# A fused attention and gated-MLP kernel: q projections begun ten units earlier, and longer DMA times in its schedule

## The chip, the cores and the metric

The kernel runs on one core of a Trainium2 chip. The metric is the device time of one execution in microseconds (us). The core's engines have queues of their own, each worked off in order: TensorE (PE; its weight loads are shown apart as PEld), VectorE (DVE), ScalarE (ACT), GpSimd (POOL), and SyncE (SP), which here only issues DMAs. They meet at semaphores.

## What is computed

For a sequence of 2048 rows of width 512, a layer norm, and then the sum of the input, an attention block of 32 heads of width 16, and an MLP gated by a ReLU, with F = 1792:

```python
qkv = x @ wqkv                       # 32 heads, 16 wide
scores = jnp.einsum("bhqd,bhkd->bhqk", q, k) * (Dh ** -0.5)
p = _softmax(scores, axis=-1)
o = jnp.einsum("bhqk,bhkd->bhqd", p, v)
...
h = (gate * (gate > 0)) * up
...
return x + _A_ref(xn, A_wqkv, A_wo) + _B_ref(xn, B_W_gate, B_W_up, B_W_down)
```

The softmax is over all 2048 keys of each of 32 heads, so there are 32 x 2048 x 2048 exponentials. They are what most of the kernel's time is arranged around.

## The kernel before

**Blocks and units.** The queries are cut into 4 pieces of 512 (`c4`), the heads into 4 groups of 8 (`gg`), and each group into two halves (`ee`) of four heads. A block is one (c4, gg, ee), and there are 32; two blocks with the same c4 and gg share one q projection and are called a pair here, numbered 0 to 15. For each block and each of the 16 key tiles of 128 there are four score tiles (one per head, 128 keys by 512 queries). Most of these tiles are gathered into units of three and two in turn: TensorE writes a unit's scores into one of two PSUM buffers (`ps_sc`, L1193), ScalarE takes the exponential of the whole unit in one instruction (L1260, into `ring`). There are 647 units. They are the clock of the schedule: dates in it are unit numbers.

**The share of VectorE.** 108 of the groups of four score tiles do not go to ScalarE. TensorE writes their scores to a PSUM bank of `ps_b`, and VectorE computes their exponentials in several instructions (L1209 from PSUM, then L1220, L1222, L1224, L1225 in SBUF, into `dring`). Which places of a block these groups take is listed in `D_POS`; how many units ahead of its place such a group is begun is `D_LEAD`.

**PV.** `pv_group` (L1149) multiplies the exponentials with v (L1169) into bank 0 of `ps_b`. Its rank in the schedule is its unit plus `PV_LAG`. The row of sums comes out of the same product, from a column of ones.

**q.** `proj_q` (L749) multiplies normalised rows with a slice of Wq into bank 1 of `ps_b`. VectorE copies the result to `qT` (L778, one buffer). Then three DMAs bring it into the layout of the scores: a write to `q_scr` in HBM (L782) and two reads into `qm` (L785, three buffers), one for each half. Pair 0 takes another way, without DMAs. A job per pair is wanted 36 units ahead of the pair's start (L1002).

**o.** `normalise` (L1089) works when a block's PV is done: VectorE copies the sums and products to `o_sb`, which lies in the storage of Wv (the profile calls it Wv, L1103); a DMA fetches the row sums into `rsum` (L1120); POOL inverts them (L1121); two DMAs bring the inverses to HBM and, repeated over partitions, back into `rb` (L1123, L1126); POOL multiplies in four parts (L1131); a DMA writes the result to `o_scr` (L1139); and after the second half of a pair one more DMA reads it back in the layout of the output product (L1145, into `oT` or into slots of `x_sb`). `out_rows` (L948) uses it, with the MLP's last product (both L726).

**MLP.** `glu` (L920) loads slices of the up and gate weights (L927, L928), multiplies (L726) and lets VectorE form h (L933, L937). The MLP, the projections and the output rows are jobs spread over the units by `spread` (L1003), whose pace is scaled by `TIGHT`. Most of these products share bank 1 of `ps_b`.

**What sets the order.** Nothing is reordered on the chip. `Graph.run` (L164) makes, when the kernel is built, one list per engine from assumed durations (`dur`), times until a result can be used (`lat`) and priorities. An operation with a date is not put ahead of that unit. For a DMA, `dur` is SP's issue and `lat` the time from there until a reader can use the data. A reader is placed where the list expects its data to be there. `SLIP` and `HOLD` are tolerances, in ns, for POOL's multiplications beside VectorE's work and for VectorE's score tiles. Where TensorE would stand idle too much, `blanks` (L257) puts in fillers: matmuls with zeros (L1310). `Graph.emit` (L349) then writes the lists out with semaphore waits. A real DMA that takes longer than its `lat` does not change the order; the engine that reads it stops there, with everything behind it.

Of the kernel before, what the change touches and what calls it, by code (L numbers as in the profile page):

```python
# [17 lines left out]
DH = 16  # L18
# [9 lines left out]

SIZES = (3, 2)
NRING = 6  # L30
PV_LAG = 2.0
PV_MIN = 0
NWS = 3
NQ = 3
NDR = 9
KD = (1, 5, 9, 13)
D_LEAD = 9.0
D_POS = (
    (), (2, 3, 8, 12), (2, 8, 11, 15), (4, 8, 11),
    (2, 6, 12), (1, 5, 9, 15), (5, 10, 14), (2, 5, 10, 11),  # L40
    (2, 3, 15), (1, 3, 4, 10), (5, 9, 15), (2, 3, 7, 12),
    (4, 6, 11), (2, 5, 9, 11), (2, 7, 12), (4, 9, 10, 13),
    (5, 10, 11), (1, 8, 9, 10), (6, 7, 10, 11), (3, 6, 13),
    (1, 8, 11, 14), (4, 8, 14), (8, 12, 15), (2, 7, 14, 15),
    (1, 8, 14), (3, 4, 11), (1, 6, 10, 13), (1, 7, 13),
    (1, 8, 10), (2, 10, 11), (1, 2, 7, 14), (1, 2, 5, 9),
)
D_BANKS = (2, 1)
D_SEQ = 0
D_AHEAD = 5  # L50
D_WAIT = 1.0
# [12 lines left out]
F_PRE = (1, 1, 1)  # L64
F_BEG = 20
F_END = 18
TIGHT = 1.0
EV = -16.0

LOG2E = 1.4426950408889634  # L70
# [31 lines left out]
class Graph:  # L102
# [2 lines left out]

    ENGS = ("PE", "ACT", "DVE", "POOL", "SP")
    SWITCH = 100.0
    SLIP = 100.0
    KEEP = 4.0
    RIDE = 100.0  # L110
    HOLD = 500.0
    WINDOW = 3400.0
    FILL = 0.72
    BLANK = 216.0
# [336 lines left out]
def bass_parallel_sum__mha_block__glu_gated_reglu__prompt_kernel(  # L451
# [16 lines left out]
    with ExitStack() as es:  # L468
        def sb(name, shape, dt):
# [35 lines left out]
        rsum = sb("rsum", [128, 2, 16], FP32)  # L505
# [32 lines left out]
             reads=[t_pid], writes=[t_pid], prio=-890)  # L538
        G.op("DVE", 100, lambda e: e.tensor_scalar(hmask[:, 1:2], pid[:, 0:1], 1.0 / 16.0, None, op0=ALU.mult),
             reads=[t_pid], writes=[t_mask], prio=-889)  # L540
        G.op("DVE", 100, lambda e: e.tensor_scalar(hmask[:, 0:1], pid[:, 0:1], -1.0 / 16.0, 1.0, op0=ALU.mult, op1=ALU.add),
             reads=[t_pid], writes=[t_mask0], prio=-888)
# [4 lines left out]
             reads=[t_id], writes=[t_id], prio=-898)  # L547
        t_vones, t_woz, t_minus = Tile(), Tile(), Tile()
        G.op("POOL", 200, lambda e: e.memset(minus[:], -1.0), writes=[t_minus], prio=10)
        t_qz = [Tile(), Tile()]  # L550
# [6 lines left out]
             reads=[t_id32], writes=[t_id32], prio=60)  # L557
# [6 lines left out]
        def dma(fn, kb, writes=(), reads=(), prio=0.0, stream=None, order=(), name="dma", after=None, dur=370.0, lat=None):  # L564
            o = G.op("SP", dur, fn, reads=reads, writes=writes, prio=prio, stream=stream or ("o", len(G.ops)),
                        lat=2000 if lat is None else lat, order=order, name=name, after=after)
            o.kb = kb if lat is None else 0.0
            return o

        x_src = x2.rearrange("(m p) d -> p m d", p=128)  # L570
        for i in range(2):
            dma(lambda e, i=i: e.dma_start(q_scr[i, :, DH:2 * DH, :], qT[:, 0, :]), 128,
                reads=[t_qt0], writes=[t_qz[i]], prio=-600)
# [35 lines left out]
        for j in range(4):  # L609
            for ee in range(2):  # L610
                dma(lambda e, j=j, ee=ee: e.dma_start(Wo_p[32 * j:32 * j + DH, ee, :], wo_src[NGG - 1, j, ee, :, :]), 16,
                    reads=[t_woz], writes=[Tile()], prio=40)
# [136 lines left out]
        def proj_q(c4, gg, prio=0.0, tile=None, sub=0, eng="DVE", slots=None):  # L749
            t = tile or Tile("pq", P_b, [1])  # L750
            prio = slots[-1] if slots else prio
            if (c4, gg) == (0, 0):
                for c0 in range(0, 384, 128):
                    first_chain(t, sub, Wq, t_wq[0], prio, c0, c0 + 128)
                first_chain(t_pro[1], 0, Wq, t_wq[0], prio, 384, 512)
            else:
                mm_chain(t, [((lambda dt=dt: Wq[:, dt, 128 * gg:128 * gg + 128]), (lambda dt=dt: xnT[:, dt, 512 * c4:512 * c4 + 512]))
                             for dt in range(DT)], [t_wq[gg], t_xnT[c4]], prio, sub=sub, slots=slots)
            tq = t_q[(c4, gg)] = Tile("q", P_q)
            if eng == "ACT":  # L760
                for tt, sb, c0, c1, up in ((t, sub, 0, 384, 0.0), (t_pro[1], 0, 384, 512, -20.0)):
                    n = (c1 - c0) // 128
                    G.op("ACT" if n == 3 else "DVE", 190 + 105 * n if n == 3 else 230, (lambda e, tt=tt, sb=sb, c0=c0, c1=c1: e.activation(
                        qm[:, tq.slot, 0, c0:c1], bank_of(tt, sb)[:, c0:c1], ACTF.Copy, scale=hmask[:, 0:1])) if n == 3 else (lambda e, tt=tt, sb=sb, c0=c0, c1=c1: e.tensor_scalar(
                        qm[:, tq.slot, 0, c0:c1], bank_of(tt, sb)[:, c0:c1], hmask[:, 0:1], None, op0=ALU.mult)),
                        reads=[tt, t_mask0], writes=[tq] if n == 3 else [t_q4], prio=prio + up)
                    o = G.ops[-1]
                    if n == 1:
                        tq.w.append(o)
                        t_after.append(o)  # L770
                    o = G.op("DVE", 100 + 130 * n, lambda e, tt=tt, sb=sb, c0=c0, c1=c1: e.tensor_scalar(
                        qm[:, tq.slot, 1, c0:c1], bank_of(tt, sb)[:, c0:c1], hmask[:, 1:2], None, op0=ALU.mult),
                        reads=[tt, t_mask], writes=[t_q1], prio=prio + 1.5)
                    o.deps[tq.w[-1]] = True
                    tq.r.append(o)
            else:
                tr = Tile("qr", P_qr)
                G.op("DVE", 610, lambda e: e.tensor_copy(qT[:, tr.slot, :], bank_of(t, sub)), reads=[t], writes=[tr], prio=prio)  # L778
                par = (4 * c4 + gg) % 2
                tqs = Tile("qs")  # L780
                tqs.r.extend(q_last[par])
                dma(lambda e: e.dma_start(q_scr[par, :, 0:DH, :], qT[:, tr.slot, :]), 128,  # L782
                    reads=[tr] + t_qz, writes=[tqs], prio=prio - 60, stream=("qw", par), dur=500, lat=2400)
                for ee in range(2):
                    dma(lambda e, ee=ee: e.dma_start(qm[:, tq.slot, ee, :], q_pick(par, ee)), 128,  # L785
                        reads=[tqs], writes=[tq] if ee == 0 else [], prio=prio - 60 + 0.1 * ee, stream=("qr%d" % ee, par), dur=500, lat=2700)
                o = G.ops[-1]
                o.order.add(tq.w[0])
                tq.w.append(o)
                q_last[par] = G.ops[-2:]  # L790
# [73 lines left out]
        def upos(c4, gg=0, ee=0, kt=0):  # L864
            x = (c4 * NGG + gg) * 2 + ee + kt / NT
            i = min(int(x), len(blocks) - 1)
            return int(starts[i] + (starts[i + 1] - starts[i]) * (x - i))
# [27 lines left out]
        o_sb = Wv[:, :, :].rearrange("p a b -> p (a b)").bitcast(FP32).rearrange("p (s q) -> p s q", s=2)  # L895
# [97 lines left out]
        def job(want, n, fn, lead=10, pace=1.0):  # L993
            jobs.append((want, n, fn, lead, pace))
# [4 lines left out]
        for c4 in range(NB):  # L999
            for gg in range(NGG):  # L1000
                if (c4, gg) != (0, 0):
                    job(upos(c4, gg) - 36, 2, lambda s, c4=c4, gg=gg: proj_q(c4, gg, slots=s))  # L1002
        def spread(a, z, items, extra):  # L1003
            pace = (z - a) / (sum(n for n, _, _, _ in items) + extra)
            pos, step = a, (z - a) / sum(n for n, _, _, _ in items)
# [22 lines left out]
        for want, n, fn, lead, pace in jobs:  # L1028
            s = []
# [10 lines left out]
        t_os, o_last = {}, [[], []]  # L1040
# [48 lines left out]
        def normalise(c4, gg, ee):  # L1089
            g = 2 * gg + ee  # L1090
            n = c4 * 8 + g
            tp = pv_tile[(c4, gg, ee)]
            to = Tile("o", P_o)
            if n == 4 * 8 - 1:
                for h in range(2):
                    o = G.op("DVE", 350, lambda e, h=h: e.tensor_copy(o_sb[:, to.slot, 256 * h:256 * h + 256], ps_b[:, 0, 256 * h:256 * h + 256]),
                             reads=[tp], writes=[to] if h == 0 else [], prio=-950, name="oev%d" % n)
# [6 lines left out]
            pr = upos(c4, gg, ee, NT) + 1  # L1104
            if (c4, gg, ee) == (NB - 1, NGG - 1, 0):
                tn, ts, tr = Tile("oT", P_oT), Tile("ls", P_b, [1]), Tile("lr", P_b, [1])
                spread_sums(lambda a, b: o_sb[:, to.slot, a:b], 0, 4, 0, lambda a, b: ps_b[:, 1, a:b], lambda p, c: ps_b[p:p + 32, 1, c:c + 128], to, ts, tr, pr + 80)
                G.op("DVE", 610, lambda e: e.tensor_tensor(oT_of(tn), ps_b[:, 1, :], o_sb[:, to.slot, :], ALU.mult),
                     reads=[tr, to], writes=[tn], prio=pr - 900)
# [6 lines left out]
            par = n % 2  # L1116
            if n >= 2:
                ts.r.extend(last_rec[n - 2][0].r)
                trr.r.extend(last_rec[n - 2][1].r)
            dma(lambda e: e.dma_start(rsum[:, par, :], o_sb[DH:128:32, to.slot, :]), 8, reads=[to], writes=[ts], prio=pr - 50, stream=("n1", n % 4), dur=600, lat=2600)  # L1120
            G.op("POOL", 3000, lambda e: e.tensor_tensor(rrec[:, par, :], rsum[:, par, :], minus[:, 0:1].to_broadcast([128, 16]), ALU.pow),  # L1121
                 reads=[ts, t_minus], writes=[trr], prio=pr - 50)
            dma(lambda e: e.dma_start(rec_scr[n].rearrange("j (i q) -> (j i) q", q=16), rrec[:, par, :]), 8,  # L1123
                reads=[trr], writes=[tsc], prio=pr - 50, stream=("n2", n % 4), dur=340, lat=1600)
            last_rec[n] = (ts, trr)
            dma(lambda e: e.dma_start(rb[:, trb.slot, :], rec_scr[n].unsqueeze(1).to_broadcast([4, 32, 512])), 256,  # L1126
                reads=[tsc], writes=[trb], prio=pr - 50, stream=("n3", n % 4), dur=580, lat=5300)
            tn = Tile("oT", P_oT)
            for k in range(N_MUL):
                w = 512 // N_MUL  # L1130
# [6 lines left out]
            tos = t_os[(c4, gg, ee)] = Tile("os")  # L1137
            tos.r.extend(o_last[par])
            dma(lambda e: e.dma_start(o_scr[par, :, ee, :, :], oT_of(tn)), 128,  # L1139
                reads=[tn], writes=[tos], prio=pr - 50, stream=("ow%d" % ee, par), dur=500, lat=2400)  # L1140
            if ee:
                tw = t_oT[(c4, gg)] = Tile("oT", P_oT)
                t = o_scr[par, :, :, :, :]
                src = bass.AP(tensor=t.tensor, offset=t.offset, ap=[(32 * 512, 8), (512, DH), (1, 512)])
                dma(lambda e: e.dma_start(oT_of(tw), src), 128,  # L1145
                    reads=[t_os[(c4, gg, 0)], tos], writes=[tw], prio=pr - 50, stream=("or", par), dur=500, lat=2600)
                o_last[par] = [G.ops[-1]]

        def pv_group(key, kt, u):  # L1149
# [206 lines left out]
```

## Time and profile before

| what | value |
|---|---|
| median of 7 runs | 776.55 us (775.56 to 779.59) |
| profiled execution | 776.03 us, of which the span of the profile is 774.2 us |
| granted TensorE clock, mean | 0.999 |
| VectorE L1209, scores from PSUM | 432 instructions, 291.6 us busy |
| GpSimd (POOL) | 162.4 us busy, 21% |
| DMA | 46.83 MB in 95757 packets, mean 60 GB/s |

The profile shows one execution. Times within it are counted in us from the start of its span. In a row of costliest groups, the figures behind the bar are the time the group was busy, the mean of one in ns, and, behind the second bar, how long the engine stood idle just before these instructions, with what ended most of that idle time. The chain of waits follows the work that ended last, back from the end: each line is a start, a length, and what it was, either an instruction or a DMA under way. A line that begins with DMA runs from its issue to the moment where its reader could go on. In the windows view a line gives a stretch, its length, the engine's busy time with the count of instructions, the TensorE clock, the share of the DMA engines and the GB/s.

### The profile page before, as it was taken

The numbers are of one execution on the slowest core, as the hardware profiler recorded it, in microseconds if no ns is written. First come the engines' busy times: TensorE is split into PE (matmuls) and PEld (weight loads), VectorE is DVE, ScalarE is ACT, GpSimd is POOL, SyncE is SP. The second block draws the span as 40 slices with busy tenths as digits, with TensorE's granted clock in tenths as the row PEclk, the third lists the DMA queues.
The fourth block names the chain that finished last, engine by engine and source line by source line (L and its number), as shares of the span: only waits on it lengthen the run. The fifth ranks groups of instructions, "written<-read, shape, count | busy, mean of one in ns | idle before, by whom it ended". The sixth has DMA issues, their size and how long they took to land.

```text
span 774.2 us, 21504 instructions
## 1 busy us (share of the span) xinstructions
PE 748.8 (97%) x9446; PEld 227.8 (29%) x9446; DVE 736.5 (95%) x1148; ACT 748.8 (97%) x662; POOL 162.4 (21%) x172
## 2 busy tenths in 40 slices
PE   8999999999999999999999999999999999999997
PEld 3322222222222322232232222222232322232333
DVE  8799999999999899999998999999999989899997
ACT  6999999999999999999999999999999999999994
POOL 3102112220212221221222021223122232121200
PEclk9999999999999999999999999999999999999999
DMA  7402121312102122232301112222230212221100
GB/s 225 134 16 60 51 62 30 78 36 64 53 28 60 48 67 57 59 82 62 84 24 56 43 49 77 57 66 67 64 81 25 63 44 66 76 69 57 36 15 29
DMA packets 95757, 46.83 MB, mean 60 GB/s; under 512 B 69936, under 2 KB 91824, under 8 KB 95664
## 3 DMA queue, kind: packets, MB, share of 16 engines
q1 hardware_dynamic: 95664, 45.46, 21.5%
q8 instruction: 74, 1.21, 0.6%
q14 instruction: 19, 0.16, 0.1%
HBM read 36.70 MB, written 8.50 MB: 58 GB/s over the span
## 4 chain that ended last, share of the span: by engine, by line
DVE 45%; PE 44%; DMA 4%; ACT 4%; issue 1%; SPq 0%; POOL 0%; DVEq 0%
DVE dring L1209 17%; PE ps_b L726 16%; PE ps_b L1169 12%; PE ps_sc L1193 12%; DVE dring L1224 7%; DVE dring L1220 4%; ACT ring L1260 4%; DVE dring L1225 4%; DVE dring L1222 4%; PE ps_b L1193 3%; DVE up_sb L933 2%; DMA qm<-q_scr 2%; DVE hT L937 2%; DVE Wv L1103 1%; DMA q_scr<-qT 1%
## 5 line engine op out<-in xcount | busy, mean ns | idle before, releaser
L1260 ACT ACTIVATE ring<-ps_sc 128x1536 bf16<-128x1536 f32 (+1 forms) x647 | 740.4, 1256 | 9.0 <-PE ps_sc L1193 4.2
L1209 DVE TENSOR_SCALAR dring<-ps_b 128x512 uint16<-128x512 f32 x432 | 291.6, 685 | 17.8 <-PE ps_b L1193 16.3
L1193 PE MATMUL ps_sc<-qm,kT 32*128 32x512 bf16 x1616 | 259.6, 384 | 2.8 <-ACT ring L1260 1.4
L1193 PE MATMUL ps_b<-qm,kT 32*128 32x512 bf16 x432 | 163.7, 384 | 6.5 <-DMA qm<-q_scr 3.1
L1169 PE MATMUL ps_b<-ring,v_aug 128*17 128x512 bf16 x1616 | 144.3, 381 | 4.4 <-DVE Wv L1103 3.4
L1121 POOL TENSOR_TENSOR rrec<-rsum,minus 128x16 f32<-128x16 f32 x30 | 96.3, 3211 | 223.9 <-DMA rsum<-Wv 223.9
L1224 DVE TENSOR_TENSOR dring<-dring 128x2048 bf16<-128x2048 bf16 x108 | 131.4, 1217 | 0.0
L1193 PEld LDWEIGHTS ps_sc<-qm,kT 32*128 32x128 bf16 x1616 | 62.0, 91 | 223.5 <-ACT ring L1260 182.1
L1131 POOL TENSOR_TENSOR x_sb<-Wv,rb 128x128 bf16<-128x128 f32 x100 | 45.9, 462 | 283.4 <-DVE dring L1220 59.7
L1169 PE MATMUL ps_b<-dring,vd 128*17 128x512 bf16 x864 | 80.6, 382 | 0.8 <-DVE dring L1224 0.2
L1169 PE MATMUL ps_b<-dring,v_aug 128*17 128x512 bf16 x864 | 78.6, 381 | 0.3
L1220 DVE TENSOR_SCALAR dring<-dring 128x2048 uint16<-128x2048 uint16 x108 | 73.9, 688 | 0.6
L1225 DVE TENSOR_SCALAR dring<-dring 128x2048 uint16<-128x2048 uint16 x108 | 73.9, 687 | 0.0
L1222 DVE TENSOR_SCALAR dring<-dring 128x2048 uint16<-128x2048 uint16 x108 | 73.8, 686 | 0.0
L726 PE MATMUL ps_b<-xnT,wus 128*32 128x512 bf16 x896 | 69.2, 384 | 1.2 <-DVE dring L1209 0.2
L726 PE MATMUL ps_b<-xnT,wgs 128*32 128x512 bf16 x896 | 68.7, 384 | 0.7 <-DVE up_sb L933 0.4
L1169 PEld LDWEIGHTS ps_b<-ring,v_aug 128*17 128x17 bf16 x1616 | 37.2, 89 | 61.0 <-issue 36.4
L1193 PEld LDWEIGHTS ps_b<-qm,kT 32*128 32x128 bf16 x432 | 38.7, 91 | 49.9 <-DVE dring L1209 27.3
L726 PE MATMUL ps_b<-Wd,hT 128*32 128x512 bf16 x672 | 48.9, 382 | 0.0
L933 DVE COPY up_sb<-ps_b 128x512 f32<-128x512 f32 x56 | 38.3, 684 | 2.2 <-PE ps_b L726 2.1
L1169 PEld LDWEIGHTS ps_b<-dring,vd 128*17 128x17 bf16 x864 | 20.5, 89 | 37.7 <-DVE dring L1225 10.9
L1169 PEld LDWEIGHTS ps_b<-dring,v_aug 128*17 128x17 bf16 x864 | 20.4, 89 | 33.1 <-issue 16.9
(109 smaller groups left out, 378.9 us busy)
## 6 DMA issues: line engine op xcount, KB each, us to landing
rb<-rec_scr SPq DMA_DIRECT2D x30, 256.0 KB
wus<-in_B_W_up_dram SPq DMA_DIRECT2D x56, 128.0 KB, 2.8
wgs<-in_B_W_gate_dram SPq DMA_DIRECT2D x56, 128.0 KB, 2.4
qm<-q_scr SPq DMA_DIRECT2D x30, 128.0 KB
o_scr<-x_sb SPq DMA_DIRECT2D x25, 128.0 KB
q_scr<-qT SPq DMA_DIRECT2D x17, 128.0 KB
xr_sb<-in_A_x_dram SPq DMA_DIRECT2D x16, 128.0 KB, 3.3
out_dram<-xn_sb SPq DMA_DIRECT2D x16, 128.0 KB, 1.7
```

Of the source, the lines that this page charges most:

```text
L726: ins = e.matmul(bank_of(tile, sub)[32 * j:32 * j + 32, :], st[:, 32 * j:32 * j + 32], mv, start=(i == 0), stop=(i == n - 1), tile_positio ...
L933: G.op("DVE", 610, lambda e: e.tensor_copy(up_sb[:, tup.slot, :], bank_of(tu)), reads=[tu], writes=[tup], prio=slots[1] + EV)
L1121: G.op("POOL", 3000, lambda e: e.tensor_tensor(rrec[:, par, :], rsum[:, par, :], minus[:, 0:1].to_broadcast([128, 16]), ALU.pow), reads=[t ...
L1131: o = G.op("POOL", 200 + 1080 // N_MUL, lambda e, a=w * k, b=w * k + w: e.tensor_tensor(oT_of(tn)[:, a:b], o_sb[:, to.slot, a:b], rb[:, tr ...
L1169: ins = e.matmul(ps_b[32 * j:32 * j + VN, 0, :], v, src[j][1](k), start=(first and k == 0), stop=(last and k == ways - 1), tile_position=( ...
L1193: return e.matmul(bank, kT[32 * j:32 * j + 32, gg, 128 * kt:128 * kt + 128], qm[32 * j:32 * j + 32, t_q[(c4, gg)].slot, ee, :], start=True ...
L1209: o = G.op("DVE", 610, lambda e, j=j, ts=ts: e.tensor_scalar(dring[:, tp.slot, 512 * j:512 * j + 512].bitcast(U16), ps_b[:, ts.slot, :], 0 ...
L1220: G.op("DVE", 600, lambda e: e.tensor_scalar(b(tm, U16), b(tp, U16), 0xFF80, None, op0=ALU.bitwise_or), reads=[tp], writes=[tm], prio=u - ...
L1222: G.op("DVE", 600, lambda e: e.tensor_scalar(b(tn, U16), b(tp, U16), 0xFF80, 1, op0=ALU.bitwise_and, op1=ALU.bitwise_or), reads=[tp], writ ...
L1224: G.op("DVE", 1140, lambda e: e.tensor_tensor(b(tm), b(tp), b(tm, I16), ALU.mult), reads=[tm, tp], writes=[tm], prio=u - 3, name="d5", loc ...
L1225: G.op("DVE", 600, lambda e: e.tensor_scalar(b(ts_, U16), b(tp, U16), float(SHIFT), None, op0=ALU.add), reads=[tp], writes=[ts_], prio=u - ...
L1260: return e.activation(ring[:, a:a + n, :], ps_sc[:, 3 * k0:3 * k0 + n, :], ACTF.Exp, scale=0.25)
```

## The change

Two named constants are new. `Q_LEAD = 46` takes the place of the number 36 in the date of the q jobs. `LATE = 900` is added to `lat` of the DMAs that TensorE's operands pass through: the write and the reads of q, the read into `rb`, and the write and the read of o. Half of it is added for the row sums and for their inverses on the way out. Other values that the lists are made from change with them: `PV_LAG`, `D_LEAD`, `TIGHT`, `SLIP`, `HOLD` and entries of `D_POS` (none of whose lists gets longer or shorter).

```diff
-PV_LAG = 2.0
+PV_LAG = 1.0
...
-D_LEAD = 9.0
+D_LEAD = 10.0
 D_POS = (
-    (), (2, 3, 8, 12), (2, 8, 11, 15), (4, 8, 11),
+    (), (2, 3, 8, 12), (2, 8, 11, 15), (4, 9, 11),
...
 D_BANKS = (2, 1)
+Q_LEAD = 46
+LATE = 900
...
-TIGHT = 1.0
+TIGHT = 0.97
...
-    SLIP = 100.0
+    SLIP = 60.0
...
-    HOLD = 500.0
+    HOLD = 400.0
...
# proj_q
                 dma(lambda e: e.dma_start(q_scr[par, :, 0:DH, :], qT[:, tr.slot, :]), 128,
-                    reads=[tr] + t_qz, writes=[tqs], prio=prio - 60, stream=("qw", par), dur=500, lat=2400)
+                    reads=[tr] + t_qz, writes=[tqs], prio=prio - 60, stream=("qw", par), dur=500, lat=2400 + LATE)
...
-  stream=("qr%d" % ee, par), dur=500, lat=2700)
+  stream=("qr%d" % ee, par), dur=500, lat=2700 + LATE)
...
# the list of jobs
-                    job(upos(c4, gg) - 36, 2, lambda s, c4=c4, gg=gg: proj_q(c4, gg, slots=s))
+                    job(upos(c4, gg) - Q_LEAD, 2, lambda s, c4=c4, gg=gg: proj_q(c4, gg, slots=s))
...
# normalise: rsum, rec_scr, rb, o_scr, oT
-  stream=("n1", n % 4), dur=600, lat=2600)
+  stream=("n1", n % 4), dur=600, lat=2600 + LATE // 2)
...
-  stream=("n2", n % 4), dur=340, lat=1600)
+  stream=("n2", n % 4), dur=340, lat=1600 + LATE // 2)
...
-  stream=("n3", n % 4), dur=580, lat=5300)
+  stream=("n3", n % 4), dur=580, lat=5300 + LATE)
...
-  stream=("ow%d" % ee, par), dur=500, lat=2400)
+  stream=("ow%d" % ee, par), dur=500, lat=2400 + LATE)
...
-  stream=("or", par), dur=500, lat=2600)
+  stream=("or", par), dur=500, lat=2600 + LATE)
```

No instruction's operands change. The orders of the engines do, and the number of filler matmuls goes from 168 to 216.

## The prediction

> **What bounds the kernel now.** I read the page's busy shares first, then the costliest groups, then ScalarE's idle time, and last the chain around each stall.
>
> ```profile
> PE 748.8 (97%) x9446; PEld 227.8 (29%) x9446; DVE 736.5 (95%) x1148; ACT 748.8 (97%) x662; POOL 162.4 (21%) x172
> L1260 ACT ACTIVATE ring<-ps_sc 128x1536 bf16<-128x1536 f32 (+1 forms) x647 | 740.4, 1256 | 9.0 <-PE ps_sc L1193 4.2
> L1193 PEld LDWEIGHTS ps_sc<-qm,kT 32*128 32x128 bf16 x1616 | 62.0, 91 | 223.5 <-ACT ring L1260 182.1
> ```
>
> Three engines are nearly full, so shares alone decide nothing. The second row is one exponential per unit: 740.4 us over 647 units is 1.144 us of ScalarE per unit. The third says that TensorE's score loads stood 182.1 us waiting for ScalarE to free a score bank: TensorE is the faster one, held to ScalarE's pace. ScalarE sets the end, and what can be gained in mid-kernel is its idle time. The windows view of ScalarE in three undisturbed stretches (length, busy):
>
> ```profile
> 75.00:420.00 345.00, 343.98 (x303) 1.00 0.21 55
> 430.00:660.00 230.00, 228.77 (x201) 1.00 0.22 57
> 715.00:755.00 40.00, 39.81 (x36) 1.00 0.09 25
> ```
>
> It idles 2.44 us in 615. The rest of its mid-kernel idle time is in four places, shown by its timeline (start, length, idle before in brackets):
>
> ```profile
> 64.86 1.02 ACT L1260 ACTIVATE ring<-ps_sc 128x1024 bf16<-128x1024 f32 x1 [0.75 <-PE ps_sc L1193]
> 66.16 1.45 ACT L1260 ACTIVATE ring<-ps_sc 128x1536 bf16<-128x1536 f32 x1 [0.28 <-PE ps_b L1193]
> ...
> 424.79 3.82 ACT L1260 ACTIVATE ring<-ps_sc 128x1536 bf16<-128x1536 f32 x3 [1.51 <-PE ps_b L1193]
> ...
> 666.33 3.46 ACT L1260 ACTIVATE ring<-ps_sc 128x1024 bf16<-128x1024 f32 x3 [0.89 <-PE ps_sc L1193]
> 670.01 2.37 ACT L1260 ACTIVATE ring<-ps_sc 128x1536 bf16<-128x1536 f32 x2 [0.22 <-PE ps_sc L1193]
> ...
> 706.72 1.03 ACT L1260 ACTIVATE ring<-ps_sc 128x1024 bf16<-128x1024 f32 x1 [0.80 <-PE ps_sc L1193]
> 708.24 2.37 ACT L1260 ACTIVATE ring<-ps_sc 128x1536 bf16<-128x1536 f32 x2 [0.49 <-PE ps_sc L1193]
> ```
>
> 0.75+0.28+1.51+0.89+0.22+0.80+0.49 = 4.94 us. In each place TensorE, working in order, had stopped just before on a DMA (0.96 us at 63.57, 1.52 at 424.02, 0.88 at 664.83, 1.26 at 705.66), and the scores behind it came late. The chain of waits shows what it stood for:
>
> ```profile
> 655.55 0.61 DVE qT L778
> 656.17 2.98 DMA q_scr<-qT
> 659.17 0.56 SPq L785
> 659.78 5.00 DMA qm<-q_scr
> 664.83 0.38 PE ps_b L1193
> ...
> 415.91 3.73 DMA o_scr<-x_sb
> 419.66 4.31 DMA oT<-o_scr
> 424.02 0.40 PE ps_b L726 x4
> ```
>
> So three stalls are q projections that come back late from HBM (pairs 1, 14 and 15 of the fifteen with a q round trip) and one is an attention output (pair 7).
>
> **The change, part by part.** Apart from fillers the built orders hold the same instructions on each engine; every cut list of D_POS keeps its length, so 647 exponentials and 108 VectorE groups stay, as does each DMA. The change only moves things, and its worth is what it does to the 4.94 us, less what the new order breaks. I count in units (one exponential each), read from the two orders.
>
> *Q_LEAD 36 to 46 and LATE on the q DMAs.* Units between the point where VectorE can begin the copy to qT and TensorE's first read of qm: before, the tightest pairs are 1, 14, 12 and 15 with 8, 8, 9 and 9. The chain (copy, write, issue, read) took 54.83 to 63.53 = 8.7 us for pair 1, 655.55 to 664.78 = 9.2 for pair 14, and 694.76 to 705.57 = 10.8 for pair 15: 7.6, 8.0 and 9.4 units, too long for 8 or 9 with any queue on VectorE. After, these pairs have 10, 15, 27 and 21 units, and the next tightest are 12 (pair 13) and 13 (pair 4). Pair 1 is a case of its own: its projection stays at unit 31 in both orders, and only its first read moves, from unit 40 to 42. That is 2 x 1.144 = 2.3 us against the 0.96 us it was short, so 1.3 us remain. I take all three q stalls as gone: 0.75+0.28+0.89+0.22+0.80+0.49 = 3.43 us.
>
> [...] The trace has 2.80 to 4.20 us for the write and 4.64 to 5.00 for the last read, so the rows decide: 3.43 us.
>
> *LATE on the o chain.* For pair 7 the oT read can be issued at unit 347 and TensorE wants it at 353: 6 units. After it is 353 and 360: 7. The one unit more is 1.1 us against 1.52 missing, so the count alone would leave 0.4 us. But at unit 347 the o_scr write stood in SP's queue behind the q_scr write of pair 9, which waited for VectorE, and shared the DMA engines with q's transfers; after, that pair's transfers are long over (unit 337) and the write is possible at 350, three units before the read. The read now stands behind the next rsum issue, which waits for the o copy of unit 353: some 1.2 us for copy and issue, then 4.31 us, is 5.5 us, 4.8 of 7 units. Bounds: 1.51 gained, or 0.4 left and so 1.1 gained; I take 1.51 for the second reason.
>
> *The queues the steps pass.* SP: the three issues of each q chain and the four or five of each o chain move with it; the smallest weight-load lead goes from 10 units to 9 (wus, 10.3 us against a median landing of 2.8), which costs nothing. qT has one buffer and qm three; no reuse comes closer than a whole pair. POOL sees the same 120 multiplies. *LATE // 2* on rsum and rec_scr only shifts work on POOL, 21% busy.
>
> *PV_LAG 2 to 1, D_LEAD, TIGHT, SLIP, HOLD, D_POS.* They reshuffle TensorE and VectorE. Explicit waits of PV on an exponential just one unit old rise from 4 to 9, with at most 0.53 us of TensorE work between the wait and the unit's end, which the score bank ahead covers, except at unit 93, where that unit's TensorE work is too long by 0.3 us. Counting each row or column group of four at 0.216 us (a run of 16 matmuls of L726 lasts 0.65 us longer than one of 4, for three groups more: 1.05 against 0.40 us in the timeline) and each change of mode at 0.105 (a score pass takes 0.32 from start to start), TensorE's total is 692.0 us in both orders: 13 fewer mode changes and 6 fewer row passes against 12 more filler groups. But it is spread otherwise. The densest 25 units hold 28.1 us before (from unit 601) and 28.9 (from 203) and 28.8 (from 525) after, where ScalarE takes 25 x 1.144 = 28.6. Before's dense stretch is inside 715 to 755, where ScalarE idled 0.19 us. So two stretches go over the line, by 0.3 and 0.2 us. Upper bound: the waits of TensorE and its loads for VectorE, 105 us in the waits view over about 670 us, come to 4.5 us in 28.6; if all lost their cover it is 4.5 each. They lie nearest to before's dense stretch, which cost almost nothing, so I take the overrun itself, 0.5 us, and 0.3 for unit 93: 0.8 us given back. What is late next once the DMA waits go is ScalarE itself.
>
> *Fillers* (168 to 216 matmuls) sit where TensorE waits: nothing. *Tail:* after the last exponential the same sums, copies and output matmuls follow: nothing, within 0.5 us either way.
>
> Sum: 4.94 - 0.8 = 4.1 us. The profiled execution took 776.03 us (span 774.2 and 1.8 around it), so 771.9 for one like it. The median, 776.55, is 0.5 higher: **772.4 us**.
>
> **Rivals.**
> 1. *A chain is still late.* Pair 1 has only 1.3 us to spare and pair 7's read now hangs on another copy. Each would keep 1.0 to 1.5 us: 773.4 with one, 774.9 with both.
> 2. *New waits replace the old.* The gap of 0.52 us at 480.45 came from VectorE and not from a DMA; six or seven more like it eat the rest: about 776. For: VectorE is 95% full and its order is new. Against: only that one such gap over 0.25 us stands in 615 us.
> 3. *Slower: TensorE becomes the bound in units 203 to 228 and 525 to 550.* With no slack there, every wait for a VectorE copy moves the scores. At 3.9 us each, of the possible 4.5: 772.4 - 0.5 + 7.8 = 779.7. It turns the gain into a loss from 2.3 us each on. For: both are over 28.6. Against: 28.1 cost nothing, and one unit of scores is always ahead.
> 4. *More gained:* the other idle falls too, by 2 us of the 2.44: 770.4 or less.
>
> That the lead does nothing is excluded for pairs 14 and 15 by the order, and holds for pair 1.
>
> **How the numbers follow.** Forecast (770.7 to 774.2) 0.53, rival 1 0.13, rival 2 0.14, rival 3 0.15, rival 4 0.05. What a measurement of this kernel can tell from no change is about 0.3%, 2.3 us: faster is below 774.2, slower above 778.9. Faster: 0.51 + half of rival 1 + rival 4 = 0.62; slower: most of rival 3, 0.12; the rest 0.26. The range leaves out 0.05 below 770.2 and about 0.14 above 777.6.
>
> **What would show it.** Right: no wait for qm or oT in TensorE's waits (before 5.5 us and 3.7 us with its loads), ScalarE's idle after unit 10 down by some 4 us, qm landing a few us before its first read. Wrong: a wait near 64 us or at the outputs of pair 7; ScalarE gaps before scores at about units 203 to 228 or 525 to 550 that end on VectorE copies; or VectorE's idle growing while ScalarE's does not fall.

## The result and the profile after

| | before | after |
|---|---|---|
| median | 776.41 us (775.23 to 780.28, 31 runs) | 770.84 us (769.95 to 773.5, 12 runs) |
| ratio after to before | | 0.9924, 95% interval 0.9911 to 0.9937 |
| profiled execution, its span | 776.03, 774.2 us | 770.03, 768.2 us |
| ScalarE idle before exponentials | 9.0 us | 4.1 us |
| ScalarE busy with exponentials | 740.4 us | 738.7 us |
| from the last exponential's end to the end | 9.7 us | 10.3 us |

The kernel became 5.6 us faster, where 4.1 was forecast. The executions differ in their mean granted TensorE clock (after: 0.998 to 0.999 in those of about 770 us, 0.994 to 0.997 in those of 771.4 to 773.5), which is why the median after lies above the profiled execution.

The page of after, busy shares and two of the costliest groups (line numbers are two higher than before):

```profile
PE 747.8 (97%) x9494; PEld 227.3 (30%) x9494; DVE 734.7 (96%) x1148; ACT 747.0 (97%) x662; POOL 159.2 (21%) x172
L1262 ACT ACTIVATE ring<-ps_sc 128x1536 bf16<-128x1536 f32 (+1 forms) x647 | 738.7, 1260 | 4.1 <-PE ps_b L1171 1.2
L1195 PEld LDWEIGHTS ps_sc<-qm,kT 32*128 32x128 bf16 x1616 | 62.0, 91 | 226.3 <-ACT ring L1262 198.7
```

The shares look the same as before. What changed is the idle time in the second row, 9.0 us before and 4.1 now. In the third row more of the wait of TensorE's score loads ends on ScalarE (198.7 us, before 182.1), but the whole of it rose only from 223.5 to 226.3 us, so this is mostly another split by what came last. In TensorE's waits there is no DMA left (before: 3.1 us on qm and 1.5 on oT, more with its weight loads). ScalarE's waits after (total, times, longest):

```profile
ACT xnT L685 <- PE ps_sc L676: 4.9, 1, 4.9
ACT ring L1262 <- PE ps_b L1171: 1.2, 3, 0.5
ACT ring L1262 <- PE ps_sc L1195: 0.9, 3, 0.6
ACT ring L1262 <- PE ps_b L1195: 0.9, 3, 0.4
```

The first line is the start of the kernel, as before. The scores' waits have gone from 6.9 us (4.2 and 2.7) to 1.8. The second line is new: before had no such wait of an exponential for a PV product (L1171 here, L1169 before; waits over 0.15 us are listed). It becomes the key to the experiments.

Mid-kernel 4.9 us of ScalarE idle went, 1.7 us of its busy time too, and the tail grew by 0.6: 6.0, the difference of the spans. The busy time shrank though the same 647 exponentials ran. Two exponentials that follow without a break overlap in the records (a 128x1536 one of before is shown for 1457 ns, and the next starts 1331 ns after it, both medians); after a break this overlap of about 0.13 us is lost. I count 65 breaks of any length on ScalarE before and 45 after. 1.7 us over 20 breaks is 0.09 us each, an estimate: a break costs more than its idle time, as far as this count explains it.

### The profile page after: what moved, and what is told of

It reads as the page before. It is cut to its first block, busy times and chain, and to the rows that moved or that the text cites. A ratio compares the mean times of both kernels' runs of the same rounds, so it can differ in the third digit from the quotient of the medians.

```text
span 768.2 us, 21611 instructions
## 1 busy us (share of the span) xinstructions
PE 747.8 (97%) x9494; PEld 227.3 (30%) x9494; DVE 734.7 (96%) x1148; ACT 747.0 (97%) x662; POOL 159.2 (21%) x172
## 3 DMA queue, kind: packets, MB, share of 16 engines
q8 instruction: 74, 1.21, 0.7%
## 4 chain that ended last, share of the span: by engine, by line
DVE 49%; PE 40%; ACT 9%; issue 1%; POOL 0%; DMA 0%; DVEq 0%
DVE dring L1211 18%; PE ps_b L728 15%; PE ps_b L1171 11%; PE ps_sc L1195 11%; ACT ring L1262 9%; DVE dring L1226 8%; DVE dring L1222 4%; DVE dring L1224 4%; DVE dring L1227 4%; DVE up_sb L935 3%; PE ps_b L1195 2%; DVE hT L939 2%; DVE Wv L1105 1%; DVE kT L811 1%; DVE stats L637 1%
## 5 line engine op out<-in xcount | busy, mean ns | idle before, releaser
L1262 ACT ACTIVATE ring<-ps_sc 128x1536 bf16<-128x1536 f32 (+1 forms) x647 | 738.7, 1260 | 4.1 <-PE ps_b L1171 1.2
L1171 PE MATMUL ps_b<-ring,v_aug 128*17 128x512 bf16 x1616 | 142.9, 381 | 3.2 <-DVE Wv L1105 2.2
L1195 PEld LDWEIGHTS ps_sc<-qm,kT 32*128 32x128 bf16 x1616 | 62.0, 91 | 226.3 <-ACT ring L1262 198.7
L1123 POOL TENSOR_TENSOR rrec<-rsum,minus 128x16 f32<-128x16 f32 x30 | 94.3, 3145 | 166.7 <-DMA rsum<-Wv 166.6
L1171 PE MATMUL ps_b<-dring,vd 128*17 128x512 bf16 x864 | 81.0, 382 | 1.0 <-DVE dring L1227 0.4
L1171 PE MATMUL ps_b<-dring,v_aug 128*17 128x512 bf16 x864 | 79.4, 382 | 0.6 <-DVE dring L1224 0.5
L728 PE MATMUL ps_b<-xnT,wus 128*32 128x512 bf16 x896 | 67.5, 383 | 0.4 <-DVE dring L1211 0.2
L1171 PEld LDWEIGHTS ps_b<-ring,v_aug 128*17 128x17 bf16 x1616 | 36.8, 89 | 56.5 <-issue 33.3
L1171 PEld LDWEIGHTS ps_b<-dring,vd 128*17 128x17 bf16 x864 | 20.6, 89 | 38.6 <-issue 12.6
L1171 PEld LDWEIGHTS ps_b<-dring,v_aug 128*17 128x17 bf16 x864 | 20.1, 89 | 32.1 <-issue 17.0
```

Of the source, the lines that this page charges most:

```text
L728: ins = e.matmul(bank_of(tile, sub)[32 * j:32 * j + 32, :], st[:, 32 * j:32 * j + 32], mv, start=(i == 0), stop=(i == n - 1), tile_positio ...
L1171: ins = e.matmul(ps_b[32 * j:32 * j + VN, 0, :], v, src[j][1](k), start=(first and k == 0), stop=(last and k == ways - 1), tile_position=( ...
L1195: return e.matmul(bank, kT[32 * j:32 * j + 32, gg, 128 * kt:128 * kt + 128], qm[32 * j:32 * j + 32, t_q[(c4, gg)].slot, ee, :], start=True ...
L1262: return e.activation(ring[:, a:a + n, :], ps_sc[:, 3 * k0:3 * k0 + n, :], ACTF.Exp, scale=0.25)
```

## The experiments

Times are medians, with those of before run on the same chip beside them. Two questions were open: whether the four DMA waits were really worth what they seemed to be, and which part of the change makes the gain, the longer lead and DMA times or the other values.

### One part at a time

**The q part alone, on before:**

```diff
-                    job(upos(c4, gg) - 36, 2, ...)
+                    job(upos(c4, gg) - 46, 2, ...)
-  stream=("qw", par), dur=500, lat=2400)
+  stream=("qw", par), dur=500, lat=2400 + 900)
-  stream=("qr%d" % ee, par), dur=500, lat=2700)
+  stream=("qr%d" % ee, par), dur=500, lat=2700 + 900)
```

> Before with the q part alone: lead 46, and 900 ns more on the three q DMAs. Units from the earliest q copy to the first read: pairs 1, 14, 15 go from 8, 8, 9 to 10, 19, 25; pair 4 falls from 14 to 9; pair 7's output read stays at 6 units. Theory W (DMA waits are the whole gain; a stall costs its idle time and the overlap lost between two exponentials, 0.12 us): the q stalls go, 3.4 + 0.6, about 772.5 us if pair 7's output still stalls, 771 if not, 773 if pair 4 now stalls. Rival R (the reshuffle by D_POS, PV_LAG, D_LEAD, TIGHT, SLIP and HOLD makes the gain): within 1 us of before, 776.

Measured: 783.04 us against 776.33; ratio 1.0056, interval 1.0029 to 1.0083. Neither theory has it. Yet the DMA waits are all but gone: TensorE's matmuls wait for none, its weight loads 0.2 us for `oT` and 0.2 us for an output in `x_sb`. Other things came instead. ScalarE waited 5.7 us, in five places of up to 1.5 us, for a PV product, and from 750.2 us on TensorE's clock was halved for 13.65 us of the profiled execution (mean clock of the whole 0.99). Three of the nine executions have a mean clock of 1.0, the other six 0.990 to 0.993; the three took 778.7 to 779.1 us, so about 4 us of the loss come and go with the clock and some 2.4 us stay.

**The o part alone, on before** (the same `lat` edits as in the change for rsum, rec_scr, rb, o_scr and oT; lead 36):

> Before with the o part alone: 900 or 450 ns more on the DMAs of the row sums and outputs, lead 36 and q times as before. Pair 7's output read has 8 units in place of 6, but seven q pairs are left with 8 units and one with 10. Theory W: the output stall goes (1.5 us), q stalls at several of these pairs, more than before: 777 to 781 us. Rival R: within 1 us of before.

Measured: 785.11 us, 1.0108 (1.0082 to 1.0134). Slower, as theory W has it, but by more than it allowed and not for its reason. (Counted in the built order as for before, five pairs have 8 units and two have 10, not seven and one.) TensorE waited for q in two places only (2.0 us, one of 1.22 us at 203.5) and 1.27 us for an output at 434.2: 3.3 us, less than the 4.6 of before. What grew is ScalarE's waits: 6.8 us for PV products, where before had none, and 12.8 for scores against 6.9. What made the scores late, if not a DMA, stays open.

**Both parts, the other values as before:**

> Lead and all the longer DMA times, with D_POS, PV_LAG, D_LEAD, TIGHT, SLIP and HOLD as before. Smallest q distance 9 units (pair 4), then 10; pair 7's output 9. Theory W: 771 to 772.5 us, nearly all of the gain. Rival R: 775 to 777.

Measured: 776.02 us against 776.33; 0.9992 (0.9976 to 1.0007). By the number alone the rival is right. The waits of ScalarE say more:

```profile
ACT ring L1260 <- PE ps_b L1169: 5.2, 6, 2.1
ACT xnT L683 <- PE ps_sc L674: 4.8, 1, 4.8
ACT ring L1260 <- PE ps_b L1193: 1.9, 3, 1.2
ACT ring L1260 <- PE ps_sc L1193: 1.1, 3, 0.6
```

The waits for scores (the third and fourth lines) fell from 6.9 to 3.0 us, with no DMA wait on TensorE: the lead and the longer times did what the prediction said. But 5.2 us went into the first line. An exponential must wait until the PV product of the unit that last used its slot of `ring` has read it. One such place, from the timeline of this kernel:

```profile
256.64 0.39 PE L1193 MATMUL ps_sc<-qm,kT 32*128 32x512 bf16 x2
...
256.96 0.40 PE L726 MATMUL ps_b<-Wo,x_sb 128*32 128x512 bf16 x4
257.18 1.25 PE L1169 MATMUL ps_b<-ring,v_aug 128*17 128x512 bf16 x20
...
257.62 2.37 ACT L1260 ACTIVATE ring<-ps_sc 128x1536 bf16<-128x1536 f32 x2 [1.21 <-PE ps_b L1169]
```

The score matmuls before it were done; five overdue PV groups stand in one run behind output products, and ScalarE stood 1.21 us until the first of them had read the ring. TensorE was not idle at all there. It had worked in the wrong order: that is why nothing of this kind shows in TensorE's waits.

**The other values alone** (after with `Q_LEAD = 36`, `LATE = 0`):

> The other values alone: after with lead 36 and no longer DMA times. q pairs 1, 12, 13, 15 and 6 have 8, 7, 8, 9 and 10 units, pair 7's output 14. Theory W: three to four q stalls, 776 to 778 us, no gain. Rival R: 771 to 772.

Measured: 789.08 us, 1.0149 (1.0125 to 1.0174). No gain, as W has it, and a larger loss: its tightest pairs have 7 and 8 units, and TensorE stood 8.2 us for q, once 4.25 us at a stretch. ScalarE waited 4.1 us for PV products besides. ScalarE through that place (stretch, length, its busy time, TensorE's clock):

```profile
576.00:581.00 5.00, 0.20 (x2) 0.88 0.28 79
581.00:584.00 3.00, 2.23 (x2) 0.50 0.21 49
584.00:588.00 4.00, 2.73 (x3) 0.67 0.22 52
```

In the two stretches after the wait the mean clock is 0.50 and 0.67, and ScalarE stands another 0.77 and 1.27 us in them.

So the change needs both halves: the lead and the DMA times remove the DMA waits, and something in the other values, together with these, keeps PV ahead of the ring.

### The waits alone, in the order of before

This takes the waits away and leaves every engine's order as it was. The reads into qm of the three late pairs take as many bytes from x, with no wait for q's write:

```diff
+FREE_Q = (1, 14, 15)
...
-  e.dma_start(qm[:, tq.slot, ee, :], q_pick(par, ee))
+  e.dma_start(qm[:, tq.slot, ee, :], x2[0:128, :] if 4 * c4 + gg in FREE_Q else q_pick(par, ee))
...
         G.run()
+        for r, w in freed:
+            r.deps.pop(w, None)
```

> Before with its order on every engine kept to the instruction; the six reads into qm of pairs 1, 14 and 15 take the same number of bytes from the input x and don't wait for the write of q, so that they land some 3 us earlier (these pairs' scores are then not of q). Theory W: the three q stalls go and the output's stays: 3.4 us of ScalarE's idle time and 0.12 us for each of five gaps, 776.3 - 4.0 = 772.3 us. Rival D (a transfer's lateness is covered anyway, and VectorE would stop TensorE in the same place): 775 to 776.5.

Measured: 772.62 us against 776.23; 0.9956 (0.9944 to 0.9968): 3.6 us, where W had 4.0 and D at most 1.3. W holds; ScalarE's idle time before exponentials fell by 3.1 us, from 9.0 to 5.9.

**Pair 7's output read freed too:**

> As the run before it, and the read of pair 7's output takes its bytes from the input x without waiting for the writes of o (that pair's output is then not of o). Theory W: all four stalls go, 4.9 us idle and 0.8 us of lost overlap, 770.6 us, the time of the changed kernel. Rival D: 774 to 776.

Measured: 772.36 us, 0.9959 (0.9944 to 0.9973). Neither. TensorE still waited 1.17 us for this read, without its having to wait for the write of o. SP's queue and the first reader, from two places of the timeline:

```profile
417.06 1.13 SPq L788 DMA_DIRECT2D qm<-q_scr  x2
418.24 0.52 SPq L1152 DMA_DIRECT2D oT<-in_A_x_dram  x1
...
422.83 0.40 PE L728 MATMUL ps_b<-Wo,oT 128*32 128x512 bf16 x4 [1.17 <-DMA oT<-in_A_x_dram]
```

The read stands behind two reads of q for pair 9 that are in no hurry themselves. So these were freed in the next run (`FREE_Q = (1, 9, 14, 15)`).

> As the run with pairs 1, 14, 15 and pair 7's output freed, and pair 9's two reads of q freed too. They stood in SP's queue waiting for their write, with the output's read behind them, so that it was issued only at 418.24 us and TensorE still waited 1.17 us for it. Theory S (SP's queue held the output back, not the wait for the write of o): the read is issued before 417.5 us, that wait goes with 1.16 us of ScalarE's idle time, about 771.2 us. Rival (the transfer itself is late, or VectorE stops TensorE in its place): 772 to 772.6.

Measured: 770.95 us against 776.46; 0.9924 (0.9907 to 0.9941). The wait is gone, and before's order without its four DMA waits is as fast as after. Its row of exponentials has 4.5 us of idle time, but hardly less busy time than the 740.4 us of before:

```profile
L1269 ACT ACTIVATE ring<-ps_sc 128x1536 bf16<-128x1536 f32 (+1 forms) x647 | 739.9, 1256 | 4.5 <-PE ps_sc L1202 1.4
```

The reason was not the one given, though. The output's read was still issued at 418.29, as two reads from x took SP 1.74 us in place of 1.13. What moved is the data. The windows view of the run before (1.17 us of wait), then of this one; the last two figures are the share of the DMA engines and GB/s:

```profile
419.00:420.00 1.00, 1.00 (x2) 1.00 0.27 89
420.00:421.00 1.00, 1.00 (x2) 1.00 0.58 182
421.00:422.00 1.00, 1.00 (x2) 1.00 0.27 96
```

```profile
419.00:420.00 1.00, 1.00 (x3) 1.00 0.89 249
420.00:421.00 1.00, 1.00 (x2) 1.00 0.02 7
421.00:422.00 1.00, 1.00 (x2) 1.00 0.00 0
```

With q's reads still under way the DMA engines work at 27 to 58% until 422; with those reads earlier (and from contiguous rows), all is done by about 420. So the place of pair 9's reads did delay the output, through the transfers and not through SP's issue. Whether time or shape of the q reads made it isn't separated here.

### What keeps the ring free

**Both parts and PV_LAG = 1**, nothing else of the other values:

```diff
-PV_LAG = 2.0
+PV_LAG = 1.0
```

> Lead and all longer DMA times, and of the other values PV_LAG = 1 alone. With PV_LAG = 2 the same had 5.3 us of ScalarE idle until a PV matmul had freed a slot of ring. Theory P (PV has to be ranked a unit earlier when other work is moved ahead of it, so that ring is freed in time): most of the 5.3 us goes, 771 to 773 us. Rival (the cut lists and the other values do it): 775 to 777.

Measured: 772.54 us against 776.23; 0.9953 (0.9941 to 0.9965). As theory P has it; the waits on PV products fell from 5.2 to 1.0 us:

```profile
ACT ring L1260 <- PE ps_sc L1193: 2.5, 3, 1.3
ACT ring L1260 <- PE ps_b L1193: 1.9, 3, 1.2
ACT ring L1260 <- PE ps_b L1169: 1.0, 2, 0.7
```

**After with PV_LAG back at 2:**

> After with PV_LAG back at 2, all else as changed. Theory P: gaps of about 1.2 us on ring come back, 4 to 6 us in all, 774 to 777 us. Rival (cut lists and other values do it): 770.5 to 772.

Measured: 777.22 us, 1.0015 (1.0003 to 1.0026): all of the gain is gone, a little slower than before, and no wait on a DMA came back. ScalarE's waits have the 5 us again:

```profile
ACT ring L1262 <- PE ps_b L1171: 6.1, 6, 1.8
```

That is not the whole loss. From the last exponential to the end it takes 13.5 us, against 10.3 in after: the last PV products wait for exponentials that VectorE finishes late, and from 768.5 us on the clock is halved for 3.41 us (mean of the whole execution 0.997, in after 0.998).

```profile
764.96 0.40 PE L1171 MATMUL ps_b<-dring,vd 128*17 128x512 bf16 x4 [0.43 <-DVE dring L1226]
765.57 0.39 PE L1171 MATMUL ps_b<-dring,vd 128*17 128x512 bf16 x4 [0.21 <-DVE dring L1227]
```

Of the 7.9 us between the two spans 5.0 are ScalarE's idle time and 3.2 this tail, less 0.4 us of busy time.

**PV_LAG = 1 alone, on before:**

> Before with PV_LAG = 1 alone. The reads of q keep their short dates: pairs 1, 4, 12 have 8, 8, 7 units and 6 and 14 have 9. Theory P with W (PV_LAG only mends ring waits, of which before has none, and can't shorten a DMA): no ring gaps, several q stalls, 776 to 781 us. Rival (PV_LAG = 1 is the gain by itself): 771 to 773.

Measured: 787.65 us, 1.0126 (1.01 to 1.0153). Not the gain by itself, as P with W has it, but far slower than expected, and with 7.4 us of waits on PV products in three places, where P had none. TensorE's matmuls waited 6.8 us for q, and 23.9 us of the profiled execution ran at half clock (mean 0.984).

**After with PV_LAG = 0.5 and with 0**, to see whether less is better:

> After with PV_LAG = 0.5. Theory P: the 1.2 us of ring gaps that after still has become smaller, and no q pair has less than 10 units: 769.5 to 772 us. Rival (every new order brings some gaps of its own, and after is a fitted set): 772 to 777.

> After with PV_LAG = 0. Theory P: no ring gaps; PV right behind its exponential can make TensorE wait for ScalarE: 769.5 to 773 us. Rival (a fitted set): 772 to 777.

Measured: 777.75 us (1.0004, 0.9989 to 1.002) at 0.5, and 771.46 us (0.9932, 0.9914 to 0.995) at 0, both against 776.46. Their waits on PV products are 6.2 and 2.7 us, after's are 1.2. So theory P in its plain form (rank PV earlier and the ring is free in time) falls: at 2, 1, 0.5 and 0 these waits are 6.1, 1.2, 6.2 and 2.7 us. PV_LAG moves every list, and which units' PV end up late does not follow its size. That the ring waits cost time is read from ScalarE's rows; why one order has them and the next has not was not found. What stands is that none of the six orders with the longer lead and all the longer times has a DMA wait on TensorE, and that much of what each pays beside after lies in what its order does to the ring. None beats after.

## Why the prediction was right, and where it was short

*What bounds.* Right: the gain is ScalarE's idle time and what hangs on it. The busy time of TensorE fell by 1.0 us and that of VectorE by 1.8, and the DMA bytes are the same.

*The q waits, 3.43 us.* Right. In before's own order their removal gave 3.6 us, of which 3.1 were idle time. The rows of the chain, 7.6 to 9.4 units long for the three pairs with 8 or 9, decided rightly: in all the orders that were run, every wait of TensorE for q over 0.15 us was of a pair with 7 to 9 units, but for one of 0.18 us with 10. Not every such pair stalled: in the o part alone two of five with 8 did. In after, pair 1's copy starts at 54.84 us and the first scores of its block follow at 64.53, with no wait.

*The o wait, 1.51 us.* Right in size: the last freed run took 1.7 us less than the one with q alone freed (1.9 less when each is counted from before on its own chip). Of the two reasons given, a place behind pair 9's write in SP's queue and DMA engines shared with its transfers, that run supports the second, for the read. In after the read is issued behind the rsum issue, as predicted, and the first weight load that uses it comes at 429.01 without a wait:

```profile
422.93 0.57 SPq L1122 DMA_DIRECT2D rsum<-Wv  x1
424.43 0.59 SPq L1147 DMA_DIRECT2D oT<-o_scr  x1
...
429.01 0.10 PEld L728 LDWEIGHTS ps_b<-Wo,oT 128*32 128x32 bf16 x4
```

*What the new order gives back, 0.8 us.* In part right, in part luck. The break expected near unit 93 is there, 0.42 us at 125.07, with TensorE busy all through. The two dense stretches, units 203 to 228 and 525 to 550, have 0.55 and 0.32 us of ScalarE idle in all, near the 0.3 and 0.2 us by which they overrun, and not 4.5. But in the first stretch the nearness is luck, since 0.47 of the 0.55 us ends on a PV product:

```profile
255.61 2.36 ACT L1262 ACTIVATE ring<-ps_sc 128x1536 bf16<-128x1536 f32 x2 [0.47 <-PE ps_b L1171]
```

The gaps at 438.83 (0.35) and 514.35 (0.34) end on the ring too, a cause that the prediction had missed. Against that, before's 0.52 at 480.45 went. In sum nothing was given back: the idle time beside the four DMA waits was 9.0 - 4.9 = 4.1 us before and is 4.1 after.

*The terms that were mis-sized.* The sum took the idle time alone, 4.9 less 0.8, and put the price of a break beyond it, and the tail, at nothing. The idle time fell by all of the 4.9 (0.8 more than forecast), 1.7 us of busy time went with it, and the tail took 0.6 more: 0.8 + 1.7 - 0.6 = 1.9 us, the distance from 4.1 to 6.0 in the profiled executions. Of the 1.7 us only some 0.5 belong to the DMA waits, since in before's order without them the exponentials were still busy for 739.9 us, with 62 breaks on ScalarE. The other 1.2 came with the new order, which has 45; the prediction had no term for it, and which of the values made it was not tested. So 770.84 lies just inside the forecast's lower end of 770.7.

*The rivals.* That a chain stays late and that TensorE becomes the bound did not happen. Rival 4 came near by its number, but the other idle time, by which it was to come, did not fall. The second rival, new waits that eat the gain, did not come in after but came in nearly every neighbour of it, and by a mechanism the prediction didn't name: it looked for waits on VectorE and found, in the orders, only PV's waits for exponentials, while the costly ones are exponentials waiting for PV. The step "PV_LAG ... reshuffle" at a cost of a few tenths was right for this set of values and says nothing of their role: with PV_LAG back at 2 the rest of the change is worth nothing.

Left open: lead and longer DMA times were not undone singly, so their shares aren't known. What D_POS, D_LEAD, TIGHT, SLIP and HOLD add was seen only as the difference between 772.54 and 770.84, and not split.

## What to carry to other kernels

In a schedule made from assumed latencies, compare each assumption with the chain's rows in the trace; a latency that was too short became a stall of the in-order engine here (0.88 to 1.52 us of TensorE in four places), and its price was the idle time of the bound engine (4.94 us of ScalarE) plus what each break cost (0.09 us by the count above, an estimate). When work is moved ahead to mend that, ask what it now stands before: here the products that free the bound engine's output buffer, whose lateness showed on no wait of the engine that was late (1.21 us of ScalarE in the place shown, none of TensorE). And judge such a change together with the values that were fitted to it: here the lead and the longer times alone gained nothing (0.9992), and the other values alone lost 1.5%.

## What the runs showed of the hardware

In some of these orders TensorE's clock halved in mid-kernel. In before and after it stays whole until after the last exponential, which ends at 764.55 and 757.97 us: it is at 1.00 up to 772.97 and 765.60. In the other values alone TensorE stood 4.25 us, and then ran at 0.5 for 6.83 us. Elsewhere no single wait of its matmuls was over 2.4 us. In the o part alone 3.41 us at half clock came near a wait of 1.22 us (mean clock 0.69 from 203 to 206 us and 0.74 from 206 to 209); in the order with PV_LAG = 1 on before it was 23.9 us in four places, with waits for q of up to 2.31 us. In the q part alone, TensorE had been busy 9.36 of the 10 us ahead of 13.65 us at half clock. But the count of matmuls had fallen, to 26 in the last 3.41 us from 41 in the 3.41 before (in before the same two stretches have 43 and 52):

```profile
740.00:750.00 10.00, 9.36 (x105) 1.00 0.08 27
743.41:746.82 3.41, 3.41 (x41) 1.00 0.02 5
746.82:750.23 3.41, 2.77 (x26) 1.00 0.13 38
750.00:753.00 3.00, 3.00 (x21) 0.54 0.15 46
753.00:756.00 3.00, 3.00 (x25) 0.50 0.00 0
756.00:759.00 3.00, 3.00 (x19) 0.50 0.00 0
759.00:762.00 3.00, 3.00 (x37) 0.50 0.02 5
762.00:765.00 3.00, 3.00 (x45) 0.69 0.00 0
765.00:771.00 6.00, 6.00 (x91) 1.00 0.00 0
```

So part of what these orders lost is not the wait but time at half clock (about 4 us in the q part alone, as its executions differ), and there a busy share of 94% over the 10 us before did not show that the clock was about to fall. That the fall in matmuls is what halves it was not tested.
